# Local-global attention and a gated mixture of attention experts: double steps, one set of PSUM banks, global scores on 544 columns

## The chip, the cores and the metric

The kernel runs on 1 core of one Trainium2 chip. The metric is the device time of one execution in microseconds (us), lower is better.

## The reference

All in fp32. Phase 1, for 8 batches x 8 heads (512 local and 32 global positions, head size 64); `band` keeps |i - j| <= 32:

```
s_g   = scale * q_g @ concat(k_g, k_l).T ;  out_g = softmax(s_g) @ concat(v_g, v_l)
s_l   = concat(scale * q_l @ k_g.T, where(band, scale * q_l @ k_l.T, -1e9))
out_l = softmax(s_l) @ concat(v_g, v_l)
x     = concat(out_g, out_l) over positions, heads side by side      # 8 x 544 x 512
```

Phase 2, per batch, with 4 experts of width 64; each position uses its two best experts:

```
w = softmax of the two largest of x @ w_gate, 0 elsewhere
for e in 0..3:  out += w[:, e] * (softmax(causal(scale * (x@wq[e]) @ (x@wk[e]).T)) @ (x@wv[e])) @ wo[e]
```

## The kernel before

**Work.** Two heads make a pair, four pairs a batch; `PAIRS` lists 32 pairs. For a pair `k`: `p1_load` and `p1_load_values` bring keys, queries and values (POOL copies shifted values and the global ones into windows of 128 rows); `p1_trans` makes `kd` (keys by windows, each followed by the 32 global keys) and `qp`; `p1_scores` (L501) writes `sp`, 32 products of 32 queries with 128 keys in two PSUM banks; `p1_softmax` (L520) is 8 passes on VectorE (L527) and 8 exponentials on ScalarE (L530); `p1_ptrans` (L539) transposes; `p1_av` (L551) gives `xq`; `p1_turn` (L572) transposes it back and `high_low` splits it into `xh` and `xl` for the products of phase 2, which run as three fp32r products (high*high, high*low, low*high). For two pairs together: `p1_global_scores` (L609, `spg`), which scores the global queries against all 640 columns of `kd` (the global keys stand there several times, and `gmask` hides the copies), `p1_global_turn`, `p1_global_av` (`xg`).

For a batch `b`: `m_v` (`pv`), `m_gates`, `m_qk` (`pqk`) for each half `c` of the experts, then per half three tiles `t` of causal scores: `m_scores` (L821, `msp`), `m_softmax` (VectorE, ScalarE, then a multiplication by weight and 1/sum on POOL, L862), `m_ptrans_units` (`mpt` into `mptw`, three buffers), `m_av` (L894, `yp`); `m_tail_scores` and what follows do the last 32 positions; `m_out` (`po`) writes 128 rows.

**Array shapes.** In the profile's rows a TensorE instruction shows rows*columns of the part of the array that it uses: `xq`, `xg`, `yt` 128*32; `sp` 64*32; `msp` 64*64; `spg`, `yp`, `tsp` 128*64; transposes, projections and `po` 128*128; `pg` (the turn of a batch's global keys and queries) 64*128.

**PSUM.** Of the 8 banks, `sc_ring` holds two double ones for `sp` and `msp`, `w_ring` four single ones for all else.

**Order.** The functions only record operations with what they read and write. `Plan.place` (L113) then sets the order: TensorE runs its operations as they were recorded; for the other engines a simulation with estimated times takes, at each moment, the ready operation with the lowest priority number (100 x step, plus `late`). Buffers are rings: an operation waits until its slot comes free. On the chip every engine runs its list in that order, held by semaphores.

**Steps.** `step(s)` (L1038 to L1111) records the work of one step, 42 in all; the pair of phase 1 is `s`, the batch of phase 2 is `b, r = divmod(s - 6, 4)`. TensorE's order in it: `xq` of pair s-2 (with `xg` in odd steps, the tail's `yt` in r = 3), in odd steps `spg` (with `yp` and the tail's scores), `sp` of pair s, one `msp` tile, then `whole(turns, products)`, a run of transposes with projections or output products spread over it, and in r = 0 and 2 a second `msp` tile.

Of the kernel before, what the change touches and what calls it, by code (L numbers as in the profile page):

```python
# [1 line left out]

# [61 lines left out]
class Plan:  # L64
# [48 lines left out]
    def place(self, log=None):  # L113
# [15 lines left out]
        while left:  # L129
# [41 lines left out]
            for b in o.bufs:  # L171
                if b.slot is None:
                    ring = b.ring
                    b.slot = min((s for s in range(ring.n) if ring.slots[s] is not None), key=lambda s: ring.slots[s])
                    ring.slots[b.slot] = None
                    ring.given += 1
                    b.tile = ring.fixed[b.slot] if ring.fixed else b.make()
# [17 lines left out]
def fused_kernel(ctx: ExitStack, tc: tile.TileContext, q_l, k_l, v_l, q_g, k_g, v_g,  # L195
# [34 lines left out]
    def ps(shape, name):  # L230
        return Buf(w_ring, lambda: psum.tile(shape, F32, tag="w", name=name, bufs=4))
# [33 lines left out]
    kds = [const.tile([128, KW], F32, name=f"kd{i}") for i in range(3)]  # L265
    kd_ring = Ring(3, fixed=kds)
# [52 lines left out]

    gmask = const.tile([128, 4, 128], F32, name="gmask")  # L320
# [19 lines left out]

    def setup_gmask():
        def f(e):
            nc.gpsimd.memset(gmask, 0.0)
            nc.gpsimd.memset(gmask[:, 1:, 96:], NEG)
        op("POOL", 800, f, w=["gmask"])
# [27 lines left out]
    X = {}  # L373
# [91 lines left out]
    def p1_trans(k):  # L465
# [5 lines left out]
        qp = buf("qp", [128, SL], 1)  # L471
# [29 lines left out]
    def p1_scores(k):  # L501
# [6 lines left out]
        def f(e):  # L508
            for t in range(4):
                for g in range(4):  # L510
                    u = 4 * t + g
                    c = col(window(u))
                    for h in range(2):
                        rows = slice(64 * h, 64 * h + 64)
                        nc.tensor.matmul(sp.t[32 * g:32 * g + 32, h, 128 * t:128 * t + 128],  # L515
                                         qp.t[rows, 32 * u:32 * u + 32], kd.t[rows, c:c + 128],
                                         start=True, stop=True)
        op("PE", 1100, f, r=[qp, kd], w=[sp])

    def p1_softmax(k):  # L520
# [3 lines left out]
        for h in range(2):  # L524
            for t in range(4):
                i = 4 * h + t
                op("DVE", 211, lambda e, h=h, t=t, i=i: nc.vector.tensor_tensor_reduce(  # L527
                    out=st.t[:, h, t], in0=sp.t[:, h, 128 * t:128 * t + 128], in1=band[:, t], scale=-SCALE, scalar=BIG,
                    op0=ALU.add, op1=ALU.min, accum_out=sm.t[:, 0, i:i + 1]), r=[sp, ("band", t)], w=[(st, i), (sm, i)])
# [9 lines left out]
    def p1_ptrans(k, h):  # L539
# [7 lines left out]
        ptw = buf("ptw", [128, SL], 3)  # L547
# [3 lines left out]
    def p1_av(k):  # L551


        pr = PR[k]
        v, sm = pr["v"], pr["sm"]
# [16 lines left out]
    def p1_turn(k):  # L572
# [8 lines left out]
        if p % 2 == 0:  # L581
            for name in ("xh", "xl"):
                X[b, p // 2, name] = buf(name, [128, 2, S], 3, F32R)
# [3 lines left out]
    def turned(prod, scale, hi_lo, reads):  # L587


        both = buf("turned", [128, 2, D], 1)  # L590
# [18 lines left out]
    def p1_global_scores(b, g):  # L609


        qb = G[b]["qb"]
        sg = buf("long", [128, 5, 128])
        sm = buf("sgm", [128, 8], 3)
        kdl = [PR[b * NP + 2 * g + j]["kd"] for j in range(2)]
        for half in range(2):
            sp = ps([128, 4 - 3 * half, 128], "spg")

            def f(e, half=half, sp=sp):
                for j in range(2):  # L620
                    p, kd, out_ = 2 * g + j, kdl[j].t, sp.t[64 * j:64 * j + 64].rearrange("p c s -> p (c s)")
                    parts = [(out_, kd[:, :512])] if half == 0 else [(out_[:, :96], kd[:, 512:608]),
                                                                     (out_[:, 96:], kd[:, 640:])]
                    for o_, k_ in parts:
                        nc.tensor.matmul(o_, qb.t[:, p, :], k_, start=True, stop=True)  # L625
            op("PE", 950 - 700 * half, f, r=[qb, *kdl], w=[sp])
            if half == 0:
                op("DVE", 610, lambda e, sp=sp: nc.vector.tensor_tensor_reduce(
                    out=sg.t[:, :4], in0=sp.t, in1=gmask, scale=-SCALE, scalar=BIG,
                    op0=ALU.add, op1=ALU.min, accum_out=sm.t[:, 0:1]), r=[sp, "gmask"], w=[(sg, 0), (sm, 0)])  # L630
            else:
                op("DVE", 210, lambda e, sp=sp: nc.vector.tensor_scalar(
                    sg.t[:, 4], sp.t[:, 0], -SCALE, None, op0=ALU.mult, op1=ALU.min, accum_out=sm.t[:, 1:2]), r=[sp],
                   w=[(sg, 1), (sm, 1)])
        op("DVE", 100, lambda e: nc.vector.tensor_reduce(sm.t[:, 2:3], sm.t[:, 0:2], axis=AX.X, op=ALU.min),
           r=[(sm, 0), (sm, 1)], w=[(sm, 2)], late=20)
        op("ACT", 825, lambda e: nc.scalar.activation(sg.t, sg.t, AF.Exp, bias=sm.t[:, 2:3], scale=-1.0,
                                                      accum_out=sm.t[:, 3:4]), r=[sg, (sm, 2)], w=[sg, (sm, 3)], late=30)
# [7 lines left out]
    def long_turn(src, key, where, part):  # L646

        n = 4 - 3 * part
        pa = ps([128, n, 128], "pga")

        def f(e):
            for j in range(n):
                nc.tensor.transpose(pa.t[:, j, :], src.t[:, 4 * part + j], ident)  # L653
        op("PE", 30 + 110 * n, f, r=[src], w=[pa])
# [3 lines left out]
        evac(lambda: pt.t[:, 4 * part:4 * part + n, :], lambda: pa.t, 128 * n, [pa], [(pt, part)])  # L658

    def p1_global_turn(b, g, part):  # L660
        long_turn(G[b, g]["sg"], "pt", G[b, g], part)

    def p1_global_av(b, g):
# [5 lines left out]
        def f(e):  # L669
            for n, w in enumerate((0, 3, 6, 9, NW)):  # L670
                for j in range(2):
                    for h in range(2):
                        c = 64 * j + 32 * h
                        nc.tensor.matmul(xg.t[c:c + 32], pt.t[:, n, c:c + 32], vs[j].t[:, h, w, :],  # L674
# [146 lines left out]
    def m_scores(b, c, t):  # L821
# [4 lines left out]
        def f(e):  # L826
            for i, at in TILES[t]:
                n = 128 * (i + 1)
                for u in range(2):
                    for x in range(2):  # L830
                        rows = slice(64 * x, 64 * x + 64)
                        q0 = 128 * i + 64 * u
                        nc.tensor.matmul(sp.t[64 * u:64 * u + 64, x, at:at + n], qt.t[rows, q0:q0 + 64],  # L833
                                         kt.t[rows, :n], start=True, stop=True)
        op("PE", 160 + 1.67 * sum(128 * (i + 1) for i, _ in TILES[t]), f, r=[kt, qt], w=[sp])

    def m_softmax(b, c, t):
# [5 lines left out]
        for k, (i, at) in enumerate(TILES[t]):  # L843
            n = 128 * (i + 1)
            for x in range(2):
                s = 2 * k + x
                op("DVE", 78 + 1.04 * n, lambda e, x=x, at=at, n=n, i=i, s=s: nc.vector.tensor_tensor_reduce(  # L847
                    out=pm.t[:, x, at:at + n], in0=sp.t[:, x, at:at + n], in1=cmask[:, 384 - 128 * i:512],
# [307 lines left out]
```

## Time and profile before

| | us |
|---|---|
| median of 3 runs (lowest to highest) | 554.78 (554.69 to 556.05) |
| the profiled execution | 553.77 |
| its span, first to last instruction | 552.0 |
| TensorE busy (share) | 512.7 (93%) |
| VectorE busy (share) | 413.8 (75%) |
| ScalarE busy (share) | 323.2 (59%) |
| POOL busy (share) | 287.7 (52%) |
| mean granted TensorE clock | 0.994 |

The span runs from the first to the last instruction; the profiled execution's own time is 1.77 us longer. Busy shares are means over stages with different limits. PE is TensorE's products and PEld its weight loads, which overlap them; DVE is VectorE, ACT ScalarE, SP SyncE. In a timeline two starts that follow each other on one engine tell its pace; the length of a product includes its way through the array, so that lengths overlap.

### The profile page before, as it was taken

Reading aid. Unit: us, or ns where it says so; the run is one execution under the profiler, and the core shown is the slowest. Engines: PE = TensorE matmul, PEld = TensorE weight load, DVE = VectorE, ACT = ScalarE, POOL = GpSimd, SP = SyncE. Lnnn points to the kernel's source line nnn. Section 1 sums busy time; section 2 is a strip of 40 time slices with the busy share of each in tenths; the row PEclk is TensorE's granted clock in tenths of the full one; section 3 lists DMA queues with packets and bytes.
Section 4 is the critical chain, followed back from the end, with each engine's and each line's share of the span. In section 5 each row is a group of like instructions: output and inputs, shape, how many; then the busy total and the mean of one; then the engine's idle time right before and its main releaser. Section 6 shows DMA issues by size and latency. Waiting matters only on the chain.

```text
span 552.0 us, 22219 instructions
## 1 busy us (share of the span) xinstructions
PE 512.7 (93%) x8796; PEld 425.4 (77%) x8796; DVE 413.8 (75%) x1713; ACT 323.2 (59%) x1146; POOL 287.7 (52%) x526
## 2 busy tenths in 40 slices
PE   4887999899999999998999999999999999999976
PEld 3666976778878887887878787788878888788754
DVE  6999879778777887779786896778877775565550
ACT  1767548866466745755675763667457464542552
POOL 6988579874193745648175642927437212231230
PEclk9989999999999999999999999999999999999989
DMA  9786585462262513533163422624122000200202
GB/s 178 144 148 129 111 160 101 86 114 42 53 149 55 95 22 70 146 70 50 25 136 87 84 34 57 145 54 78 22 48 80 2 2 2 78 2 1 77 2 95
DMA packets 190792, 41.83 MB, mean 76 GB/s; under 512 B 186080, under 2 KB 186080, under 8 KB 190688
## 3 DMA queue, kind: packets, MB, share of 16 engines
q1 hardware_dynamic: 174448, 29.12, 28.8%
q10 hardware_dynamic: 16240, 11.29, 6.7%
q8 instruction: 69, 1.13, 0.9%
q14 instruction: 35, 0.29, 0.2%
HBM read 31.47 MB, written 8.91 MB: 73 GB/s over the span
## 4 chain that ended last, share of the span: by engine, by line
PE 65%; DVE 11%; ACT 9%; DMA 5%; POOL 4%; issue 3%; SPq 2%; POOLq 0%; DVEq 0%; ACTq 0%
PE pqk L704 13%; PE pv L741 8%; PE po L984 7%; PE msp L833 6%; PE xq L564 5%; PE mpt L886 5%; PE yp L905 4%; PE sp L515 4%; POOL v L240 3%; PE pt L545 3%; PE spg L625 2%; ACT st L530 2%; DMA v<-in_v_l_dram 2%; PE xp L579 2%; PE pga L653 2%
## 5 line engine op out<-in xcount | busy, mean ns | idle before, releaser
L240 POOL COPY v<-v 32x512 f32<-32x512 f32 (+2 forms) x192 | 116.3, 606 | 46.6 <-DMA v<-in_v_l_dram 36.1
L862 POOL TENSOR_SCALAR pm<-pm,msm,gate 128x512 f32<-128x512 f32 (+3 forms) x128 | 76.9, 614 | 119.8 <-DVE msm L856 86.3
L530 ACT ACTIVATE st<-st,sm 128x128 f32<-128x128 f32 x256 | 100.4, 395 | 35.2 <-DVE sm L527 26.9
L240 POOL COPY v<-vg 32x640 f32<-32x640 f32 (+1 forms) x96 | 65.9, 686 | 38.5 <-PE xg L674 26.8
L851 ACT ACTIVATE pm<-pm,msm 128x512 f32<-128x512 f32 (+3 forms) x128 | 70.6, 554 | 22.9 <-DVE msm L847 22.8
L847 DVE CUSTOM_DVE_ANT_0 pm<-msp,cmask 128x512 f32<-128x512 f32 (+3 forms) x128 | 56.9, 486 | 11.2 <-PE msp L833 11.2
L527 DVE CUSTOM_DVE_ANT_0 st<-sp,band 128x128 f32<-128x128 f32 x256 | 58.1, 285 | 9.4 <-PE sp L515 9.4
L886 PE MATMUL mpt<-ident,pm 128*128 128x128 f32 x320 | 48.1, 276 | 7.1 <-DVE kt L240 3.4
L886 PEld LDWEIGHTS mpt<-ident,pm 128*128 128x128 f32 x320 | 36.5, 141 | 16.2 <-POOL pm L862 5.5
L530 ACT ACTIVATION_READ_ACCUMULATOR st<-st,sm 128x1 f32 x256 | 48.7, 190 | 0.0
L833 PE MATMUL msp<-kt,qt 64*64 64x384 f32 (+3 forms) x512 | 46.1, 448 | 0.5 <-DVE qt L240 0.5
L515 PE MATMUL sp<-kd,qp 64*32 64x128 f32 x2048 | 39.6, 283 | 3.9 <-issue 1.8
L564 PEld LDWEIGHTS xq<-v,ptw 128*32 128x32 f32 x2048 | 30.7, 111 | 14.8 <-issue 6.2
L564 PE MATMUL xq<-v,ptw 128*32 128x64 f32 x2048 | 36.2, 223 | 5.6 <-ACT ptw L238 2.7
L905 PE MATMUL yp<-mptw,vt 128*64 128x128 f32 x640 | 40.1, 278 | 0.3 <-issue 0.3
L704 PE MATMUL pqk<-xh,wk_hi 128*128 128x272 f32 x128 | 39.6, 309 | 0.3 <-DVE xl L604 0.3
L545 PE MATMUL pt<-ident,st 128*128 128x128 f32 x256 | 36.4, 274 | 3.5 <-DVE xl L250 3.2
L704 PE MATMUL pqk<-xh,wq_hi 128*128 128x272 f32 x128 | 39.7, 310 | 0.0
L238 ACT COPY mptw<-mpt 128x512 f32<-128x512 f32 (+1 forms) x51 | 23.9, 487 | 26.2 <-PE mpt L886 25.6
L741 PE MATMUL pv<-wv_hi,xh 128*128 128x260 f32 x128 | 38.6, 301 | 0.7 <-DVE xl L250 0.7
L905 PEld LDWEIGHTS yp<-mptw,vt 128*64 128x64 f32 x640 | 36.2, 139 | 1.7 <-issue 0.7
L704 PE MATMUL pqk<-xl,wq_hi 128*128 128x272 f32 x128 | 36.9, 288 | 0.0
(166 smaller groups left out, 1365.9 us busy)
## 6 DMA issues: line engine op xcount, KB each, us to landing
out_dram<-ot ACTq DMA_DIRECT2D x32, 256.0 KB, 2.1
v<-in_v_l_dram SPq DMA_DIRECT2D x62, 120.0 KB, 3.2
kn<-in_k_l_dram SPq DMA_DIRECT2D x109, 64.0 KB, 2.7
qn<-in_q_l_dram SPq DMA_DIRECT2D x109, 64.0 KB, 2.4
v<-in_v_l_dram SPq DMA_DIRECT2D x59, 32.0 KB, 2.5
vg<-in_v_g_dram SPq DMA_DIRECT2D x21, 64.0 KB, 2.2
qn<-in_q_l_dram ACTq DMA_DIRECT2D x5, 128.0 KB, 2.7
ot<-in_q_g_dram SPq DMA_DIRECT2D x8, 64.0 KB, 2.2
```

The source lines that it names most:

```text
L240: ENG[e].tensor_copy(out, in_)
L515: nc.tensor.matmul(sp.t[32 * g:32 * g + 32, h, 128 * t:128 * t + 128], qp.t[rows, 32 * u:32 * u + 32], kd.t[rows, c:c + 128], start=True, ...
L527: op("DVE", 211, lambda e, h=h, t=t, i=i: nc.vector.tensor_tensor_reduce(out=st.t[:, h, t], in0=sp.t[:, h, 128 * t:128 * t + 128], in1=ban ...
L530: op("ACT", 385, lambda e, h=h, t=t, i=i: nc.scalar.activation(st.t[:, h, t], st.t[:, h, t], AF.Exp, bias=sm.t[:, 0, i:i + 1], scale=-1.0, ...
L564: nc.tensor.matmul(xq.t[32 * g:32 * g + 32, t, h, :], pts[h].t[:, 32 * u:32 * u + 32], v.t[:, h, window(u), :], start=True, stop=True)
L704: nc.tensor.matmul(pp.t, w[:, ch, cols], x(part, ch)[:, n], start=(ch == 0 and w is hi and part == 0), stop=(ch == NCH - 1 and part == 1))
L741: nc.tensor.matmul(pv.t, x(part, ch)[:, 128 * i:128 * i + 128], w[:, ch, :], start=(ch == 0 and part == 0 and w is hi), stop=(ch == NCH - ...
L833: nc.tensor.matmul(sp.t[64 * u:64 * u + 64, x, at:at + n], qt.t[rows, q0:q0 + 64], kt.t[rows, :n], start=True, stop=True)
L851: op("ACT", 280 + 0.83 * n, lambda e, x=x, at=at, n=n, s=s: nc.scalar.activation(pm.t[:, x, at:at + n], pm.t[:, x, at:at + n], AF.Exp, bia ...
L862: op("POOL", 240 + 0.83 * n, lambda e, x=x, at=at, n=n, i=i, s=s: nc.gpsimd.tensor_scalar(pm.t[:, x, at:at + n], pm.t[:, x, at:at + n], sm ...
L886: nc.tensor.transpose(pt.t[:, k, :], pm.t[:, x, at + 128 * j:at + 128 * j + 128], ident)
L905: nc.tensor.matmul(yp.t[64 * x:64 * x + 64, 128 * i:128 * i + 128], vt.t[:, j, 64 * (2 * c + x):64 * (2 * c + x) + 64], flat[:, where[x, i ...
```

## The change

- **Double steps.** `step(d)` records two pairs and half a batch of phase 2; 21 steps in place of 42. TensorE's order: `xq` of both pairs of the step before, `xg` (and `yt`); `sp` of both pairs; `yp` (with the tail's scores), `spg`; a run of 128*128 work; two `msp` tiles; a second 128*128 run, with the transposes of the pairs' scores; one `msp` tile. In step 2 the first batch's `pv` come ahead of the scores of pairs 4 and 5.
- **Banks.** One ring of eight single banks; a score tile takes two of them. Buffers: `kd` 3 to 2; `qp`, `turned` 1 to 2; `ptw` 3 to 4; `mptw` stays at 3.
- **Global scores.** The copies of the global keys in windows 1 to 3 are left out: 416 + 128 columns, no `gmask`; the transposes take blocks of 128, 96, 96, 96 and 128 columns, and the last 32 rows of the first block get a copy of their own.
- **End.** The last batch's tiles come earlier, its multiplications may go to VectorE, its last `yp` is made in two halves, and the tail's output goes first.

Cut to its core:

```diff
-    sc_ring, w_ring = Ring(2, loose=True), Ring(4, loose=True)
+    banks = [psum.tile([128, 512], F32, name=f"bank{i}", bufs=1) for i in range(8)]
+    ring = Ring(8, loose=True, fixed=banks)
...
     def scores(name):
-        return Buf(sc_ring, lambda: psum.tile([128, 2, 512], F32, tag="sc", name=name, bufs=2))
+        return [ps([128, 512], name) for _ in range(2)]
...
     def p1_global_scores(b, g):
...
+                    if half == 0:
+                        parts = [(o_[:, :128], kd[:, :128]),
+                                 (o_[:, 128:].rearrange("p (c s) -> p c s", s=96),
+                                  kd[:, 128:512].rearrange("p (c s) -> p c s", s=128)[:, :, :96])]
+                    else:
+                        parts = [(o_[:, :96], kd[:, 512:608]), (o_[:, 96:], kd[:, 640:])]
+                    for to, k_ in parts:
+                        nc.tensor.matmul(to, qb.t[:, p, :], k_, start=True, stop=True)
...
+    CHUNKS = ((0, 128), (128, 96), (224, 96), (320, 96), (416, 128))
...
     def m_softmax(b, c, t):
...
+                engs = "POOL|DVE" if b == B - 1 and c == 1 else "POOL"
...
+    def step(d):
+        plan.prio = 200 * d
+        odd = d % 2
+        new = (d - 2 - odd) // 2
+        mid, old = new - 1, new - 2
+        pairs = [k for k in (2 * d, 2 * d + 1) if k < NK]
+        done = [k for k in (2 * d - 2, 2 * d - 1) if 0 <= k < NK]
...
+        for k in done:
+            p1_av(k)
+            first.append(lambda k=k: p1_turn(k))
...
+        def scores_of_pairs():
+            for k in pairs:
+                p1_scores(k)
+                p1_softmax(k)
+            if not odd and has(old):
+                m_av(old, 1, M[old, "turn"] if end else None)
+            if odd and has(mid):
+                m_av(mid, 0)
+                m_tail_scores(mid)
+            if pairs:
+                b, p = PAIRS[pairs[0]]
+                p1_global_scores(b, p // 2)
...
+        if odd:
+            first += units((mid, 1, 2), (mid, 1, 1), (mid, 1, 0))
+            if has(new):
+                products = project(0, 2)[:2] if new == 0 else project(new, 1)
+        else:
+            first += units((mid, 0, 1), (mid, 0, 0))
+            if has(old):
+                products = [lambda i=i: m_out(old, i) for i in range(4)]
...
+        if d == 2:
+            whole(first, [])
+            whole([], products)
+            scores_of_pairs()
+        else:
+            whole(first, products, 3 if odd else 0, 0 if odd else 2)
+        if odd:
+            tiles((new, 0, 2), (new, 0, 1))
+        elif mid == B - 1:
+            tiles((mid, 1, 1), (mid, 1, 0))
+        else:
+            tiles((mid, 1, 2), (mid, 1, 1))
...
+        for k in pairs:
+            second += [lambda k=k: p1_ptrans(k, 0), lambda k=k: p1_ptrans(k, 1)]
...
+        if odd:
+            if has(mid):
+                second += [lambda: m_tail_turn(mid, 0), lambda: m_tail_turn(mid, 1)]
+            second += units((new, 0, 2))
+            if has(new):
+                products = project(new, 2)[2 if new == 0 else 0:]
+        elif has(new):
+            products = project(new, 0 if new > 0 else 1)
...
+        whole(second + turned_late, products)
+        if odd:
+            tiles((new, 0, 0), *([(new, 1, 2)] if new == B - 1 else []))
+        elif mid != B - 1:
+            tiles((mid, 1, 0))
```

## Rows read from the trace of the kernel before

**Rows 1.** Part 1 of the page: busy microseconds of each engine, share of the span, instructions.
```profile
PE 512.7 (93%) x8796; PEld 425.4 (77%) x8796; DVE 413.8 (75%) x1713; ACT 323.2 (59%) x1146; POOL 287.7 (52%) x526
```

**Rows 2.** Busy time of each engine in four stretches of the span: start and end, length, then for each engine busy us and instructions, the granted TensorE clock, the DMA engines' share, GB/s.
```profile
0.00:69.00 69.00, 53.75 (x1164) 45.04 (x1167) 58.64 (x258) 39.13 (x158) 53.81 (x104) 0.98 0.75 142
69.00:441.60 372.60, 357.99 (x6534) 297.73 (x6524) 298.40 (x1241) 232.26 (x833) 211.49 (x380) 1.00 0.38 76
441.60:524.40 82.80, 81.43 (x932) 68.08 (x932) 48.21 (x182) 40.80 (x126) 17.61 (x34) 1.00 0.07 27
524.40:552.00 27.60, 19.55 (x189) 14.56 (x184) 8.56 (x34) 10.99 (x32) 4.79 (x8) 0.94 0.14 49
```

**Rows 3.** Part 4 of the page: the chain of work that ended last, by engine.
```profile
PE 65%; DVE 11%; ACT 9%; DMA 5%; POOL 4%; issue 3%; SPq 2%; POOLq 0%; DVEq 0%; ACTq 0%
```

**Rows 4.** What TensorE waited for in 69 to 441.6 us: engine, tile and line that waited, what it waited for, us in total, times, the longest.
```profile
PE mpt L886 <- DVE kt L240: 3.4, 4, 1.2
PE pt L545 <- DVE xl L250: 3.2, 5, 0.6
PE po L984 <- ACT ot L238: 2.4, 4, 0.6
```

**Rows 5.** Timeline, 255.9 to 258.2 us: start, length, engine, line, operation, tiles and shapes, count, and in brackets the idle time before and what ended it.
```profile
256.16 0.29 PE L704 MATMUL pqk<-xl,wq_hi 128*128 128x272 f32 x1
...
257.04 0.43 DVE L240 COPY kt<-pqk 128x272 f32<-128x272 f32 x1
...
257.62 0.41 PE L886 MATMUL mpt<-ident,pm 128*128 128x128 f32 x2 [1.17 <-DVE kt L240]
```

**Rows 6.** Timeline of TensorE, 43.9 to 50.9 us (the columns of group 5, here and in all timelines below).
```profile
44.11 1.10 PE L564 MATMUL xq<-v,ptw 128*32 128x64 f32 x64 [2.05 <-ACT ptw L238]
45.02 0.74 PE L674 MATMUL xg<-v,longt 128*32 128x64 f32 x40
...
50.85 0.39 PE L741 MATMUL pv<-wv_hi,xh 128*128 128x260 f32 x1 [0.67 <-DVE xl L250]
```

**Rows 7.** Timeline of TensorE, 56.8 to 58.9 us.
```profile
56.84 1.10 PE L564 MATMUL xq<-v,ptw 128*32 128x64 f32 x64
57.88 1.16 PE L515 MATMUL sp<-kd,qp 64*32 64x128 f32 x64
```

**Rows 8.** Timeline of TensorE, 257 to 260.6 us.
```profile
259.12 0.29 PE L704 MATMUL pqk<-xh,wq_lo 128*128 128x272 f32 x1
259.24 0.29 PE L704 MATMUL pqk<-xl,wq_hi 128*128 128x272 f32 x1
259.46 1.10 PE L564 MATMUL xq<-v,ptw 128*32 128x64 f32 x64
```

**Rows 9.** Timeline of TensorE, 210 to 213.5 us: the global scores of two pairs, then the products of a batch with its values.
```profile
210.97 1.38 PE L625 MATMUL spg<-kd,qgbd 128*64 128x512 f32 x12
212.13 1.61 PE L905 MATMUL yp<-mptw,vt 128*64 128x128 f32 x25
```

**Rows 10.** Groups of instructions by line and shape: line, engine, operation, tiles, shapes, count, busy us, mean ns of one, idle us before them and what ended it.
```profile
L238 ACT COPY longt<-pga 128x128 f32<-128x128 f32 x18 | 4.8, 267 | 16.1 <-PE pga L653 15.9
```

**Rows 11.** The same view, VectorE.
```profile
L240 DVE COPY mptw<-mpt 128x512 f32<-128x512 f32 x36 | 24.2, 685 | 4.4 <-PE mpt L886 3.7
L568 DVE TENSOR_TENSOR xn<-xq,sm 128x512 f32<-128x512 f32 x32 | 22.0, 687 | 12.2 <-PE xq L564 12.1
...
L498 DVE STREAM_TRANSPOSE qp<-qn 128x512 f32<-128x512 f32 x28 | 19.7, 703 | 0.0
L495 DVE STREAM_TRANSPOSE kd<-kn 128x480 f32<-128x480 f32 x28 | 18.8, 672 | 1.2 <-DMA kn<-in_k_l_dram 1.0
...
L847 DVE CUSTOM_DVE_ANT_0 pm<-msp,cmask 128x256 f32<-128x256 f32 x32 | 12.2, 420 | 0.0
...
L847 DVE DVE_READ_ACCUMULATOR2_ANT msm<- 128x1 f32 x128 | 10.6, 83 | 0.0
...
L847 DVE CUSTOM_DVE_ANT_0 pm<-msp,cmask 128x128 f32<-128x128 f32 x32 | 8.0, 286 | 5.1 <-PE msp L833 5.1
...
L591 DVE TENSOR_SCALAR turned<-xg,sgm 128x128 f32<-128x128 f32 x16 | 5.5, 342 | 0.0
...
L496 DVE STREAM_TRANSPOSE kd<-kn 128x32 f32<-128x32 f32 x28 | 4.7, 168 | 0.0
```

**Rows 12.** Timeline, the last 33 us.
```profile
526.20 1.11 PE L926 MATMUL tsp<-kt,qtbd 128*64 128x512 f32 x8
...
532.86 1.19 PE L886 MATMUL mpt<-ident,pm 128*128 128x128 f32 x6 [2.39 <-POOL pm L862]
...
535.36 1.29 PE L965 MATMUL yt<-vt,longt 128*32 128x64 f32 x40 [0.77 <-DVE longt L240]
...
536.58 3.21 PE L905 MATMUL yp<-mptw,vt 128*64 128x128 f32 x40
...
539.72 0.33 PE L597 MATMUL tt<-ident,turned 128*128 128x128 f32 x1
...
547.96 1.76 ACTq L991 DMA_DIRECT2D out_dram<-ot  x4
```

**Rows 13.** Busy time in 535 to 537 us (the columns of group 2).
```profile
535.00:537.00 2.00, 1.64 (x44) 1.50 (x46) 0.50 (x2) 0.00 (x0) 0.00 (x0) 0.50 0.04 8
```

**Rows 14.** The chain that ended last in order of time, 430 to 445 us: start, us, what.
```profile
436.00 2.23 PE yp L905 x40
```

More of the change, by code (lines that the diff above doesn't have):

```diff
@@ L1 @@
 from contextlib import ExitStack
+import math
 import concourse.bass as bass
@@ L264, in fused_kernel @@
     KW = 32 * (NB + NB // 3)
-    kds = [const.tile([128, KW], F32, name=f"kd{i}") for i in range(3)]
-    kd_ring = Ring(3, fixed=kds)
+    kds = [const.tile([128, KW], F32, name=f"kd{i}") for i in range(2)]
+    kd_ring = Ring(2, fixed=kds)
     NW = NB - 2
@@ L612, in p1_global_scores @@
         qb = G[b]["qb"]
-        sg = buf("long", [128, 5, 128])
+        sg = buf("long", [128, 640])
         sm = buf("sgm", [128, 8], 3)
         kdl = [PR[b * NP + 2 * g + j]["kd"] for j in range(2)]
-        for half in range(2):
-            sp = ps([128, 4 - 3 * half, 128], "spg")
+        for half, n in ((0, 416), (1, 128)):
+            sp = ps([128, n], "spg")
             def f(e, half=half, sp=sp):
                 for j in range(2):
[L621 to L634, printed above, removed]
@@ L892, in m_ptrans_units, with m_av @@
         return units
[L894 removed]
+    def m_av(b, c, between=None):
         vt = M[b, "v"]
         pts = {i: (M[b, c, t, "pt"], M[b, c, t, "where"]) for t in range(3) for i, _ in TILES[t]}
[L897 to L908 removed]
         if c == 0:
@@ L911, in m_av, with f @@
         y = M[b, "yo"]
-        high_low(lambda part: y[part].t[:, c, :], lambda: yp.t, 512, [yp], (y[0], c), (y[1], c))
+        for some in ((0, 1), (2, 3)) if between else (range(4),):
+            n0, n = 128 * some[0], 128 * len(some)
+            yp = ps([128, n], "yp")
+            def f(e, some=some, yp=yp, n0=n0):
+                for i in some:
+                    pt, where = pts[i]
+                    flat = pt.t.rearrange("p a j q -> p (a j) q")
+                    for j in range(i + 1):
+                        for x in range(2):
+                            nc.tensor.matmul(yp.t[64 * x:64 * x + 64, 128 * i - n0:128 * i - n0 + 128],
+                                             vt.t[:, j, 64 * (2 * c + x):64 * (2 * c + x) + 64],
+                                             flat[:, where[x, i, j], :], start=(j == 0), stop=(j == i))
+            op("PE", 235 * sum(i + 1 for i in some), f, r=[vt, *{id(pts[i][0]): pts[i][0] for i in some}.values()], w=[yp])
+            high_low(lambda part, n0=n0, n=n: y[part].t[:, c, n0:n0 + n], lambda yp=yp: yp.t, n, [yp],
+                     (y[0], (c, n0)), (y[1], (c, n0)))
+            if between and n0 == 0:
+                between()
     def m_tail_scores(b):
@@ L954, in m_tail_turn @@
     def m_tail_turn(b, part):
-        long_turn(M[b, "ptail"], (b, "pttail"), M, part)
+        long_turn(M[b, "ptail"], (b, "pttail"), M, part, [(128 * j, 128) for j in range(5)])
     def m_tail_av(b):
@@ L994, in m_out @@
     def m_out(b, i):
-        y = M[b, "yo"]
-        out_tile(y, lambda part, c: y[part].t[:, c, 128 * i:128 * i + 128],
+        y = [(t, (c, n0)) for t in M[b, "yo"] for c in range(2) for n0 in ((0, 256) if b == B - 1 and c == 1 else (0,))
+             if n0 == 0 or i > 1]
+        out_tile(y, lambda part, c: M[b, "yo"][part].t[:, c, 128 * i:128 * i + 128],
                  [(out[b, 128 * i:128 * i + 128, :], slice(0, 128))])
@@ L1002, in m_out_tail, with whole @@
                  [(out[4 * g + r, SL:, :], slice(32 * r, 32 * r + 32)) for r in range(4)])
-    NK = len(PAIRS)
-    LAG = 6
-    def at(k):
-        return 0 <= k < NK
-    def has(b):
-        return 0 <= b < B
-    def whole(turns, products):
-        n = max(len(turns), 1)
+    NK, NG = len(PAIRS), len(PAIRS) // 2
+    def whole(turns, products, last=0, skip=0):
+        n = max(len(turns) - last - skip, 1)
         done = 0
@@ L1117, in fused_kernel @@
     p1_trans(0)
+    p1_trans(1)
     setup_bands()
-    setup_gmask()
     p1_load_values(0)
-    for s in range(LAG + 4 * B + 4):
-        step(s)
+    for d in range(2 * B + 5):
+        step(d)
         for name, when in (("masks", 3), ("v", 1), ("k", 3), ("q", 4), ("o", 6)):
-            if s == when:
+            if d == when // 2:
+                plan.prio = 100 * when
                 setup(name)
```

242 lines of the change are left out of this document (114 added, 128 removed).

## The prediction

> **What bounds the kernel now.** Read the busy times first [rows 1]: TensorE works in 93% of the span, VectorE next. Then the span in four stretches [rows 2]: in the long middle one (69.00 to 441.60) TensorE is busy for 357.99 of 372.60 us at full clock, so 14.6 us are idle; at the start 15.3 of 69.00, in the last 27.60 us 8.0. The chain that ended last [rows 3] is TensorE for 65%. So TensorE in program order is the bound from 69 us on, and a time falls by less work there, by fewer waits inside its order, or at the two ends. VectorE is busy for 298.40 of the same 372.60 us (80%): it is the next bound.
>
> What ends TensorE's waits in the middle [rows 4] is mostly an evacuation: its next product needs a PSUM bank that VectorE or ScalarE has not yet emptied. One of them in order of time [rows 5]: the last projection product starts at 256.16, the copy of `kt` out of its bank starts at 257.04, and only then the transposes of `mpt` go (257.62), though the two `sc` double banks were not needed then.
>
> **The profiled execution** took 553.77 us (span 552.0 and 1.77 around it); the median of the three runs shown is 554.78, 1.0 above. Sums below are differences, set against the median. A measurement of this kernel tells about 0.3% (1.7 us) from no change.
>
> **Part 1, fewer changes of array shape.** Leaving a shape costs TensorE time in which nothing starts. `xq` followed by `xg` of the same shape takes 45.02-44.11 = 0.91 us [rows 6]; the same `xq` followed by `sp` takes 57.88-56.84 = 1.04 [rows 7]: 0.13 for the change. After projection products the next one starts 0.12 us on, after the last one another shape starts 259.46-259.24 = 0.22 on [rows 8]: 0.10. I take 0.10, ends 0.09 and 0.13. How many go away follows from `step`, since TensorE's order is the program's. One batch (four steps before) has 6+5+5+5 = 21 changes: `xq`, then in odd steps the 128*64 products, `sp`, `msp`, the 128*128 run, in r = 0 also `pg` and in r = 0, 2 a second `msp`. After, two double steps: odd `xq, sp, yp/tsp/spg, 128*128, msp, 128*128, msp` = 7, even the same with `pg` = 8. So 15, 6 fewer per batch, 48 in 8 batches, and by the same count 2 more at the ends: 50 x 0.10 = **-5.0 us** (-4.5 to -6.5), all on TensorE.
>
> **Part 2, 544 columns.** The `spg` run takes 212.13-210.97 = 1.16 us [rows 9] for four passes each of 512, 96 and 32 columns, 2560 in all: 0.45 ns per column. The three blocks of 32 masked columns go, 4 x 96 = 384 columns: 0.17 us x 16 = -2.8; four more instructions a run eat a little: **-2.6 us**. No row shows a moving operand that skips columns (96 of every 128): if each of the 288-column passes took twice its 0.13 us, the part would cost 4 x 0.13 x 16 = 8.3 and end at +5.7. I take -2.6, since contiguous ones are all that is near. VectorE's pass over the scores and ScalarE's exponential shrink with the columns, and 16 copies of 267 ns [rows 10] come in for the first block's last 32 rows; these two engines have room, and TensorE has the double step to cover them. Transposes of 96 columns may go faster than the 128 they replace: 0, at best -1.3 (16 x 3 x 0.11 x 1/4).
>
> [...]
>
> **Part 3, waits in the middle.** The bodies with both phases are 13 double steps (d = 3 to 15), so 14.6 us is 1.1 us of idle TensorE per double step. Eight banks in one set take away the waits of [rows 5]'s kind, which [rows 4] put at 3.4+3.2+2.4 = 9.0 us. Products also get further from what they wait for: the transposes of a pair's scores come half a double step after the scores, the last tile's transposes end a whole run. But the head of a double step is new: two `xq`, `xg`, two `sp`, all quick, all filling banks. TensorE runs them in 2 x 0.91 + 0.57 + 1.16 = 3.6 us [rows 6, 7] (0.57: the 40 of `xg` at the pace of the 64 of `xq`) before the second `sp` starts. In that time VectorE must empty the small `msp` tile (2 x 420 + 2 x 286 + 4 x 83 = 1.74 us), two `xq` (2 x 687) and `xg` (342) [rows 11]: 3.5 us. That only just holds, and TensorE's stop there shifts whatever is queued behind it. In even double steps two banks are short besides: `mptw` has three slots, all taken by the second half's tiles until `m_av(old, 1)`, so the transposes of tile (new, 0, 2) stand in PSUM over the step's end. I take 0.8 us per double step in place of 1.1: **-4 us** (-12 with no waits of that kind, +23 by the rival below). VectorE's load rises to about 298/363 = 82%, still under TensorE's.
>
> The queues: SyncE issues the same loads with the same priorities, 16 for a double step's keys and queries, whose two slots come free half a double step before they are needed again; POOL (211.49 of 372.60 us) copies values as before, now for two pairs in a row; ScalarE's queue issues the outputs one by one after their copies. None of them ends a TensorE wait in [rows 4].
>
> **Part 4, start.** Up to 69 us TensorE waits for loads, VectorE (58.64 of 69.00 us busy) and POOL (53.81) [rows 2]. The change puts the first `pv` before pairs 4 and 5. Before, `xq` of pair 3 starts at 44.11 after 2.05 us of idle time and `pv` at 50.85 after 0.67, waiting for its `xl` on VectorE, which has pair 5's softmax as well [rows 6]. With `pv` in front that last idle and that of `sp` go: **-2 us** (-5 to +4: pairs 2 and 3 are now transposed later, and `kd` has two buffers).
>
> **Part 5, end.** [...] The last output was four DMAs, 1.76 us of issuing on ScalarE's queue after 547.96 [rows 12]; now it is one, so three quarters go: 1.3. Half-products of `yp` let its evacuation run beside TensorE: 0.3 to 0.5. Together **-4 us** (-6 to +1).
>
> **Sum:** -5.0-2.6-4-2-4 = -17.6, so 554.8-17.6 = 537 us.
>
> **Rivals.**
> 1. Forecast: 537, own range 529 (part 3 at -12) to 546 (part 3 at 0, the start 5 us later). Chance 0.56.
> 2. The waits only move: a bank is free, but the same VectorE and ScalarE work is late at the head; 1.1 us per double step stay, nothing at the start: 554.8-5.0-2.6-4 = 543. For it: VectorE at 80%, and the waits of [rows 4] end with its work. Chance 0.18.
> 3. Slower: the head of the double step. If VectorE comes there with one pair's transposes (672+168+703 ns) and two 512-column copies (2 x 685) to do [rows 11], 2.9 us late, both `sp` wait as long, in each of 13: idle 38 us in place of 14.6, 543+23 = 566. It decides from (14.6+11.6)/13 = 2.0 us per double step on; at that point the time is 555. Against it: work that is late here is not late again behind. Slower by over 0.3%: 0.14; about even: 0.07.
> 4. The 288-column passes at half speed, the rest as forecast: 537+8.3 = 545. Chance 0.05. [...]
> That the change doesn't do what it says has little room: order and column counts are in the program.
>
> **The numbers.** Faster by over 0.3%: 0.56+0.18+0.05 = 0.79; same 0.07; slower 0.14. The range goes from 527 (the forecast's lower end with part 5 at -6) to 554, which takes in rivals 2 and 4 and the better half of no change.
>
> **What would show it.** Right: 133 or so changes of shape in place of 183 (not counting the value product of the last rows, whose 64 columns show as a change in both); a `spg` run near 1.0 us; TensorE idle about 0.8 us per double step, with few waits on `kt`, `xl` and `ot`; `pv` before the sixth pair's `sp`; full clock in the last 20 us and one issue at the end. Wrong: waits of 2 us and more ahead of the second `sp` or `yp`, ended by VectorE's `xn` or `pm`; a VectorE without idle time in the middle; `spg` above 1.16 us; `pv` later than 51 us.

## The result, and the profile after

The changed kernel takes 559.78 us (median of 14 runs, 555.73 to 563.83), the kernel before 555.39 (14 runs beside it): ratio 1.0079, 95% interval 1.0052 to 1.0105. It is slower by 0.8%; 537 with a range to 554 was predicted. The profiled execution took 559.0 us, its span is 557.2.

Part 1 and part 3 of the page (in part 3: queue, kind, packets, MB, share of the DMA engines), then the same four stretches as [rows 2], the last with its own end:

```profile
PE 505.6 (91%) x8860; PEld 436.0 (78%) x8860; DVE 410.2 (74%) x1732; ACT 318.2 (57%) x1148; POOL 284.9 (51%) x521
...
q8 instruction: 70, 1.15, 0.9%
```
```profile
0.00:69.00 69.00, 53.59 (x992) 44.29 (x992) 53.86 (x235) 32.85 (x136) 56.18 (x108) 0.93 0.75 145
69.00:441.60 372.60, 344.86 (x6377) 301.72 (x6377) 289.58 (x1227) 227.66 (x830) 207.60 (x373) 0.99 0.37 76
441.60:524.40 82.80, 79.16 (x1218) 68.25 (x1218) 53.26 (x222) 41.40 (x141) 16.17 (x32) 1.00 0.04 15
524.40:557.20 32.80, 27.97 (x279) 21.78 (x275) 13.47 (x50) 16.27 (x44) 4.95 (x9) 0.99 0.21 74
```

TensorE has 7.1 us less to do than in [rows 1], 505.6 against 512.7, and the kernel is still slower: TensorE stands still more. In the middle stretch it is idle for 372.60-344.86 = 27.7 us, against 14.6 in [rows 2]. VectorE, which the slower rival had in mind, is busy for less of that stretch than before (289.58 against 298.40).

What TensorE waits for in 104 to 445 us, in the form of [rows 4]. All PSUM tiles are called `bank` now, so the line tells what waits: L522 is `sp`, L689 `xg`, L988 `yt`, L928 `yp`, L575 `xq`.

```profile
PE bank L522 <- issue: 12.1, 10, 1.8
PE bank L689 <- issue: 3.8, 3, 1.4
PE bank L988 <- issue: 2.7, 2, 1.6
PE bank L928 <- issue: 1.3, 3, 0.8
PE bank L575 <- issue: 1.2, 1, 1.2
PE bank L590 <- issue: 0.3, 1, 0.3
```

Not one wait on VectorE or ScalarE is left: the kind of [rows 4] is gone. All that stands here is "issue", time for which the profile shows nothing that TensorE waits for. Over the whole span it is 28 us. The head of one double step, in the columns of the timelines above (the profile has two passes for each of these float32 matmuls, 32 products of a pair's `sp` as `x64` in [rows 7], so `x128` is 64 matmuls):

```profile
186.28 1.00 PE L575 MATMUL bank<-v,ptw 128*32 128x64 f32 x57
187.10 0.67 PE L689 MATMUL bank<-v,longt 128*32 128x64 f32 x33
189.16 0.32 PE L689 MATMUL bank<-v,longt 128*32 128x64 f32 x7 [1.39 <-issue]
189.40 1.96 PE L522 MATMUL bank<-kd,qp 64*32 64x128 f32 x121
192.61 0.42 PE L522 MATMUL bank<-kd,qp 64*32 64x128 f32 x7 [1.25 <-issue]
192.96 1.75 PE L928 MATMUL bank<-mptw,vt 128*64 128x128 f32 x28
```

The stops fall inside a product, in the middle of a tile whose bank is already held: after 33 of the 40 passes of `xg`, after 121 of the 128 of `sp`. From one stop's end to the next one's lie 7+121 = 128 passes and 192.61-189.16 = 3.45 us. Each pass is one weight load and one matmul (2048 of each on L522 in the page), so that is 256 instructions.

Where the time went, from the first `pv` of the second batch and of the last one: before, then after.

```profile
103.02 0.36 PE L741 MATMUL pv<-wv_hi,xh 128*128 128x260 f32 x1
...
480.54 0.37 PE L741 MATMUL pv<-wv_hi,xh 128*128 128x260 f32 x1
```
```profile
109.18 0.39 PE L756 MATMUL bank<-wv_hi,xh 128*128 128x260 f32 x1
...
492.13 0.39 PE L756 MATMUL bank<-wv_hi,xh 128*128 128x260 f32 x1
```

To the second batch +6.2 us; from there to the last 382.9 against 377.5, +5.4; from there to the end of the span 557.2-492.1 = 65.1 against 552.0-480.5 = 71.5, -6.4. The end gained, the start and the middle lost.

At the start TensorE waits twice for nearly 3 us for ScalarE's exponential of the global scores (L643), and after each of these waits the granted clock is low. Timeline around the first, and the clock (the column before the last two) in 71.00 to 75.20 and 92.30 to 95.70:

```profile
71.17 0.77 PE L667 MATMUL bank<-ident,long 128*128 128x128 f32 x5 [2.94 <-ACT long L643]
71.87 3.58 PE L575 MATMUL bank<-v,ptw 128*32 128x64 f32 x128
```
```profile
71.00:75.20 4.20, 4.03 (x133) 3.87 (x137) 1.70 (x4) 0.64 (x4) 0.00 (x0) 0.60 0.71 116
...
92.30:95.70 3.40, 3.40 (x18) 3.40 (x16) 1.32 (x2) 1.11 (x3) 1.16 (x2) 0.50 0.90 190
```

Two `xq` take 3.58 us there, 1.92 in the chain of waits in mid-kernel: at a granted clock of 0.60 in the first window and 0.50 in the second, 1.00 in 185 to 193 us, what follows the pause is stretched too. Ahead of the first `pv` both kernels have low stretches (0.57 in 41 to 49 us, before 0.66 in 36 to 41).

The last 20 us, beside [rows 12, 13]: the wait ahead of `mpt` is 0.24 us (2.39 before), that ahead of `yt` 0.88 (0.77 before), and, as the prediction asked, the clock in 541 to 545 is 1.00 and the last output is one issue of 0.34 us in place of four in 1.76.

```profile
540.18 0.97 PE L904 MATMUL bank<-ident,pm 128*128 128x128 f32 x5 [0.24 <-POOL pm L880]
...
542.89 0.77 PE L988 MATMUL bank<-vt,longt 128*32 128x64 f32 x40 [0.88 <-DVE longt L255]
```
```profile
541.00:545.00 4.00, 3.03 (x66) 2.26 (x66) 2.20 (x8) 0.93 (x6) 0.00 (x0) 1.00 0.00 0
```

### The profile page after: what moved, and what is told of

It is laid out like the page before. It is cut to its first block, busy times and chain, and to the rows that moved or that the text cites. A ratio compares the mean times of both kernels' runs of the same rounds, so it can differ in the third digit from the quotient of the medians.

```text
span 557.2 us, 22376 instructions
## 1 busy us (share of the span) xinstructions
PE 505.6 (91%) x8860; PEld 436.0 (78%) x8860; DVE 410.2 (74%) x1732; ACT 318.2 (57%) x1148; POOL 284.9 (51%) x521
## 3 DMA queue, kind: packets, MB, share of 16 engines
q8 instruction: 70, 1.15, 0.9%
## 4 chain that ended last, share of the span: by engine, by line
PE 84%; issue 6%; DVE 5%; ACT 3%; DMA 1%; POOL 0%; SPq 0%; POOLq 0%; ACTq 0%; DVEq 0%
PE bank L719 16%; PE bank L756 9%; PE bank L1007 9%; PE bank L848 7%; PE bank L928 6%; PE bank L522 6%; PE bank L904 6%; PE bank L575 6%; PE bank L552 4%; PE bank L590 3%; PE bank L636 3%; PE bank L667 3%; PE bank L689 2%; PE bank L767 1%; PE bank L949 1%
## 5 line engine op out<-in xcount | busy, mean ns | idle before, releaser
L862 DVE CUSTOM_DVE_ANT_0 pm<-bank,cmask 128x512 f32<-128x512 f32 (+3 forms) x128 | 55.1, 488 | 19.2 <-PE bank L848 13.4
L534 DVE CUSTOM_DVE_ANT_0 st<-bank,band 128x128 f32<-128x128 f32 x256 | 57.0, 286 | 12.4 <-PE bank L522 11.9
L522 PE MATMUL bank<-kd,qp 64*32 64x128 f32 x2048 | 38.6, 280 | 17.3 <-issue 17.3
L522 PEld LDWEIGHTS bank<-kd,qp 64*32 64x32 f32 x2048 | 30.5, 108 | 22.7 <-issue 21.4
L904 PE MATMUL bank<-ident,pm 128*128 128x128 f32 x320 | 45.4, 276 | 0.8 <-POOL pm L880 0.7
L552 PE MATMUL bank<-ident,st 128*128 128x128 f32 x256 | 39.1, 279 | 4.1 <-ACT st L537 3.4
L848 PE MATMUL bank<-kt,qt 64*64 64x256 f32 (+3 forms) x512 | 41.6, 441 | 0.0
L928 PE MATMUL bank<-mptw,vt 128*64 128x128 f32 x640 | 39.8, 276 | 1.5 <-issue 1.5
L719 PE MATMUL bank<-xh,wq_hi 128*128 128x272 f32 x128 | 39.8, 311 | 0.0
L719 PE MATMUL bank<-xh,wk_hi 128*128 128x272 f32 x128 | 39.4, 308 | 0.0
L928 PEld LDWEIGHTS bank<-mptw,vt 128*64 128x64 f32 x640 | 35.0, 137 | 5.6 <-issue 3.8
L756 PE MATMUL bank<-wv_hi,xh 128*128 128x260 f32 x128 | 38.6, 302 | 0.0
L552 PEld LDWEIGHTS bank<-ident,st 128*128 128x128 f32 x256 | 29.3, 140 | 11.8 <-ACT st L537 8.1
L575 PEld LDWEIGHTS bank<-v,ptw 128*32 128x32 f32 x2048 | 32.5, 118 | 6.9 <-DVE qt L255 2.3
```

Source lines behind the costliest of these rows:

```text
L522: nc.tensor.matmul(sp[h].t[32 * g:32 * g + 32, 128 * t:128 * t + 128], qp.t[rows, 32 * u:32 * u + 32], kd.t[rows, c:c + 128], start=True, ...
L552: nc.tensor.transpose(pt.t[:, t, :], st.t[:, h, t], ident)
L575: nc.tensor.matmul(xq.t[32 * g:32 * g + 32, t, h, :], pts[h].t[:, 32 * u:32 * u + 32], v.t[:, h, window(u), :], start=True, stop=True)
L719: nc.tensor.matmul(pp.t, w[:, ch, cols], x(part, ch)[:, n], start=(ch == 0 and w is hi and part == 0), stop=(ch == NCH - 1 and part == 1))
L756: nc.tensor.matmul(pv.t, x(part, ch)[:, 128 * i:128 * i + 128], w[:, ch, :], start=(ch == 0 and part == 0 and w is hi), stop=(ch == NCH - ...
L848: nc.tensor.matmul(sp[x].t[64 * u:64 * u + 64, at:at + n], qt.t[rows, q0:q0 + 64], kt.t[rows, :n], start=True, stop=True)
```

## The experiments

**Theory F**: TensorE runs out of its own instructions. They come by DMA during the run, 70 packets on queue q8, 1.15 MB or 16.4 KB each: TensorE's 2 x 8860 instructions make 253 a packet, in the kernel before 2 x 8796 in 69 packets 255. A head of `xq`, `xq`, `xg` (`yt`), `sp`, `sp` is 592 to 672 short instructions in one piece; before, the longest such piece was 288. **Theory V**, the prediction's slower rival: VectorE comes late with the banks of the head. A third possibility, that any other order moves the time, is what the last two runs are for.

### The pace of short matmuls by itself

```
for k in range(24): nc.tensor.matmul(warm, a[:, :128], b, ...)   # 512 columns
for k in range(20): sp(short)        # 20 x 32 matmuls in the form of sp
av(wide, 320)                        # in the form of yp
for k in range(10): sp(mixed); av(wide, 16)
for k in range(2): sp(mixed)
```

> Not the reference's computation: loads two tiles, runs matmuls with no wait among them, writes one tile to all of the output. After 24 wide matmuls to warm up: 640 matmuls of the form of sp in one piece (2560 instructions of TensorE), then 320 of the form of yp, then ten times 32 of sp and 16 of yp, then 64 of sp. Theory F: the piece of sp runs at 3.4 to 3.5 us for each 64 matmuls (256 instructions), 34 to 35 us in all, with an idle stretch ended by 'issue' in each block; the piece of yp has none; the mixed piece has next to none. Theory V: 64 of sp take about 2.1 us as in the kernel, 21 us in all, with no idle time, for nothing but TensorE takes part.

Timeline of TensorE in the long piece of `sp` form, then one turn of the mixed piece:

```profile
27.80 2.67 PE L220 MATMUL short<-b,a 64*32 64x128 f32 x175
31.87 2.02 PE L220 MATMUL short<-b,a 64*32 64x128 f32 x128 [1.40 <-issue]
35.87 2.02 PE L220 MATMUL short<-b,a 64*32 64x128 f32 x128 [1.99 <-issue]
...
47.06 2.25 PE L220 MATMUL short<-b,a 64*32 64x128 f32 x128 [0.17 <-issue]
50.51 2.02 PE L220 MATMUL short<-b,a 64*32 64x128 f32 x128 [1.21 <-issue]
...
61.97 1.39 PE L220 MATMUL short<-b,a 64*32 64x128 f32 x81 [1.71 <-issue]
```
```profile
98.37 1.16 PE L220 MATMUL mixed<-b,a 64*32 64x128 f32 x64
99.45 1.97 PE L226 MATMUL wide<-b,a 128*64 128x128 f32 x32
101.35 1.16 PE L220 MATMUL mixed<-b,a 64*32 64x128 f32 x64
```

No product waits for another engine or for a bank, and TensorE stops after every 128 passes exactly. From 31.87 to 61.97 a block of 256 instructions takes 30.10/8 = 3.76 us (3.45 to 4.00), of which some 2.0 are work. The mixed piece passes 192 instructions in 2.98 us, or 256 in 3.97, and does not stop; nor does the wide one. The whole piece took 35.5 us (63.28-27.80, where the wide one starts), a little more than the 34 to 35 of F; a piece without stops would be V's 21. The page has 23 packets on q8 within the run of this small kernel, 0.38 MB or 16.5 KB each; TensorE's 2 x 3056 instructions make 266 a packet, near the 256 (128 pairs) from stop to stop.

```profile
q8 instruction: 23, 0.38, 1.1%
```

When they come is in the trace as well. One block, cut at the start and at the end of its packet (the columns of [rows 2], here without ScalarE):

```profile
31.87:32.97 1.10, 1.10 (x80) 1.10 (x83) 0.00 (x0) 0.00 (x0) 1.00 0.00 0
32.97:34.43 1.46, 0.92 (x67) 0.65 (x48) 0.00 (x0) 0.00 (x0) 1.00 0.06 11
34.43:35.87 1.44, 0.00 (x0) 0.00 (x0) 0.00 (x0) 0.00 (x0) 1.00 0.00 0
```

TensorE goes on at 31.87; the next packet starts 1.1 us later and takes 1.45 (11 GB/s for 1.46 us are its 16 KB); 1.44 us after its end TensorE goes on again. In the nine stops of the piece these three times are 1.05 to 1.13, 0.94 to 1.45 and 1.34 to 1.48 us, so that a block is long where its packet is slow. In the changed kernel each of the 25 stops on "issue" ends 1.2 to 1.6 us after the end of a packet on q8. That is F's mechanism and not only its pace.

### The products put between: the order of the head

```
         def scores_of_pairs():
-            for k in pairs:
-                p1_scores(k)
-                p1_softmax(k)
             if not odd and has(old):
                 m_av(old, 1, M[old, "turn"] if end else None)
...
                 p1_global_scores(b, p // 2)
+            for k in pairs:
+                p1_scores(k)
+                p1_softmax(k)
```

> The changed kernel with one order turned round: in every double step the 128x64 products (yp, tsp, spg) are recorded between the xq/xg products and the scores of the two pairs, and no longer behind these scores. Same instructions, same number of changes of array shape, same eight banks. Theory F (TensorE runs out of its own instructions: a block of 256 of them is not had faster than about 3.45 us, and xq, xg, sp, sp are 592 to 672 short ones in one piece): the run of short ones is cut into 208 to 288 and 256, the idle time of TensorE ended by 'issue' falls from 28 us to 10 to 14 us, and the time from about 559 to 542 to 548 us. Theory V (VectorE frees the scores' banks too late): the scores come later against VectorE's queue, which helps too, 3 to 5 us, but the idle time ended by 'issue' stays over 20 us.

542.64 us, ratio to before 0.9771 (0.9731 to 0.981): 17 us faster than the changed kernel, by order alone. The waits on "issue" went from 28.3 to 12.0 us. TensorE's other named waits grew by 3 us, and its busy time fell from 505.6 to 501.3, with less of the start at the low clock. The largest rows:

```profile
PE bank L689 <- issue: 4.9, 4, 1.5
...
PE bank L522 <- issue: 3.5, 3, 1.7
...
PE bank L988 <- issue: 2.1, 2, 1.1
...
PE bank L575 <- issue: 1.2, 1, 1.2
```

V's small gain, with "issue" still over 20 us, is not what came.

### The same order at the start alone

```
+            early = d < 4
+            if not early:
+                of_pairs()
...
+            if early:
+                of_pairs()
```

> The same order as in the run before, in the first four double steps alone. Global scores then reach ScalarE ahead of the pairs' 16 exponentials. If the two waits of 3 us for the exponential of the global scores at 71 and 92 us, and the low clock behind them, are what the start lost: 5 to 8 us faster than the changed kernel, 551 to 554 us, with the idle time ended by 'issue' in the middle unchanged at some 20 us. If the start lost its time to instructions or to loads: within 2 us of the changed kernel.

558.4 us, ratio 1.0049 (1.0017 to 1.0082): some 1.4 us less than the changed kernel, with overlapping intervals. The waits on the exponential fell from 6.8 to 1.3 us and the clock in 71.00 to 75.20 was 1.00, but 4.3 us of waits on POOL's normalization came in their place:

```profile
PE bank L904 <- POOL pm L880: 4.3, 3, 3.6
...
PE bank L667 <- ACT long L643: 1.3, 1, 1.3
```

The wait was found rightly and its worth was not: behind it stood another. In the trace the second batch comes at 106.74 us, 2.4 earlier than in the changed kernel, where 5 to 8 were expected.

### Longer short runs in the kernel before

```
+        if at(s):
+            p1_scores(s)
+            p1_softmax(s)
         if at(s) and s % 2 == 1:
...
             m_av(old, 1)
-        if at(s):
-            p1_scores(s)
-            p1_softmax(s)
```

> The kernel before with one order turned round the other way: in every step the pair's scores are recorded ahead of spg, yp and tsp, so that in odd steps xq, xg (and yt) and sp stand in one piece of 336 to 416 short instructions. Old PSUM buffers, same number of changes of shape. Theory F: idle time ended by 'issue' appears in odd steps only, 0.5 to 1.4 us in about half of them, 5 to 15 us in all, and the kernel gets slower by 3 to 10 us (558 to 565). Theory V: no idle time of that kind, the time within 2 us of before.

557.91 us, ratio 1.0034 (1.0008 to 1.006), 1.9 us slower: under the 3 to 10 expected, but the waits are there, in the kernel with the old banks, 9.0 us on "issue" in all against 2.6, six of them inside `sp` where there was one:

```profile
PE sp L515 <- issue: 7.6, 6, 1.6
```

Five of the six fell in odd steps, where F puts them (pieces of 336 to 416 instructions do not all hold a whole block); the sixth, in an even step, is the one that the kernel before has. TensorE's other waits are 7 us shorter in all, which hides much of it in the time.

### One more cut

```
+        def narrow():
+            if done:
+                b, p = PAIRS[done[0]]
+                p1_global_av(b, p // 2)
...
                 m_tail_scores(mid)
+            if late:              # d >= 4 and not end
+                narrow()
             if pairs:
```

> As the run with the products between (542.6 us), with xg and yt put behind these products too, ahead of spg: xq, xq | yp, tsp | xg, yt | spg | sp, sp. No piece of short instructions is then longer than 256; two changes of array shape more in each of some 15 double steps. Theory F: idle time ended by 'issue' falls from 12.0 us to 2 to 5 us, the added changes cost 30 x 0.10 = 3 us, so 535 to 541 us. If the rest of those waits were something else than instructions: the 12 us stay and the time is 543 to 547 us.

542.58 us: no gain, against 535 to 541. Waits on "issue" did fall, from 12.0 to 5.6 us. Two rows of the waits that are left:

```profile
PE bank L522 <- issue: 4.1, 8, 1.7
...
PE bank L848 <- DVE qt L255: 3.0, 3, 1.4
```

The trace has 23 more changes of shape, 2.3 us at the 0.10 of part 1; the mixture's scores wait 2.3 us longer for `qt` (0.7 with the order before) and 0.5 longer for ScalarE. That is most of the 6.4 gained, as far as the waits tell. From here on instructions are not the only thing that ends a wait.

### The old division of the banks

```
+    sc_ring, w_ring = Ring(4, loose=True, fixed=banks[:4]), Ring(4, loose=True, fixed=banks[4:])
```

(In the placing of operations, one that needs two banks of a ring also waits until two are free.)

> As the run with the products between (542.6 us), with the eight banks split as in the kernel before: four for scores, four for the rest. Tells what one set of eight is worth. If VectorE's late frees were what bounded the kernel before (part 3 of the prediction): 4 to 10 us slower, with waits of TensorE on VectorE and ScalarE back. Theory F in its strict form, where banks matter little beside instructions: within 3 us of 542.6. In both, idle time ended by 'issue' stays at 10 to 14 us.

554.42 us, ratio 0.9972 (0.995 to 0.9994): 11.8 us slower than with one set of eight (11.2 by the two ratios), more than the 4 to 10 expected. So in this order one set of eight banks is worth what part 3 gave as its far end (-12), and the strict form of F falls: banks matter beside instructions. In the order of the changed kernel their worth was not measured. The waits on "issue" add up to 12.1 us as without the division; six waits on `xl` are back:

```profile
PE bank L1010 <- DVE xl L268: 4.7, 6, 1.0
```

All waits on VectorE are 9.4 us, 3.0 without the division. That names 6.4 of the 11.8; TensorE's busy time is longer too (509.9 against 501.3 for the same instructions), and why stays open.

### 544 columns alone

```
-        for half in range(2):                  # in the kernel before
+        for half, n in ((0, 416), (1, 128)):   # and its products, copies and exponential
```

> The kernel before with the global scores on 544 columns and nothing else of the change. Prediction's part 2: -2.6 us, 552 to 554 us. If moving 96 of every 128 columns halves TensorE's speed: +5.7 us or more, 561. Its spg of 416 columns tells which: about 160 ns a pass if the columns cost the same, about 320 if half speed.

551.75 us, ratio 0.9924 (0.9892 to 0.9956): -4.2 us (-6.0 to -2.4), 2.6 expected. The run of global scores, from its start to that of `yp`:

```profile
213.44 1.23 PE L621 MATMUL spg<-kd,qgbd 128*64 128x128 f32 x16
214.44 2.43 PE L905 MATMUL yp<-mptw,vt 128*64 128x128 f32 x40
```

1.00 us, 1.16 in [rows 9]: 0.16 x 16 = 2.6 us on TensorE, as summed. Moving 96 of every 128 columns shows no cost: four passes each of 128, 288, 96 and 32 columns are 2176, or 0.46 ns per column, 0.45 in part 2. Transposes of 96 columns show a mean of 282 ns in the changed kernel, those of 128 the same, and both start 0.11 us apart: no gain there.

### The start mended

```
-            second += units((new, 0, 2))
+            second += units(*([(new, 0, 2)] if new else []))
-            first += units((mid, 0, 1), (mid, 0, 0))
+            first += units(*([(mid, 0, 2)] if mid == 0 else []), (mid, 0, 1), (mid, 0, 0))
```

> As the run with the products between (542.6 us), but the transposes of the first batch's first mixture tile are moved one half step later (from the end of double step 3 to the head of step 4), since TensorE waits 3.9 us there for GpSimd's normalised probabilities. If that wait is on the path: 2 to 4 us faster (539 to 541). If only the place of the wait moves: within 1 us of 542.6.

536.72 us, ratio 0.9648 (0.9617 to 0.9679): 5.9 us faster than the products between alone, and the best of all here. TensorE reaches the second batch at 104.34 us and the last at 470.48:

```profile
104.34 0.39 PE L756 MATMUL bank<-wv_hi,xh 128*128 128x260 f32 x1
...
470.48 0.39 PE L756 MATMUL bank<-wv_hi,xh 128*128 128x260 f32 x1
```

With the order alone these were 106.39 and 475.08. So 2 us came at the start and another 2.5 between the two, for which no single wait stands and whose cause stays open; the spans differ by 4.5 us, the medians by 5.9.

### Work added at the stop, and elsewhere

```
+    def extra(d):            # double steps 4 to 15
+        for _ in range(2):
+            nc.tensor.matmul(pad.t[:64], ident[:, :64], cmask, start=True, stop=True)
```

> The changed kernel with more work and none moved: in double steps 4 to 15 two matmuls of 128x64 by 512 columns (8 instructions, 4 passes of 0.43 us by the pace of the warm-up passes, 1.72 us) whose result nobody reads stand between xq/xg/yt and the scores of the pairs. 12 x 1.72 = 20.6 us of added work, and 12 changes of shape. Theory F: while the wide passes run the next block of instructions arrives, so the waits of the scores on 'issue' fall by 9 to 14 us and the time grows by 6 to 12 us over 559. Theory V, or any in which the order of the products is what mattered: it grows by 20 to 23 us.

> The control of the run before: the same 20.6 us of added work in the same double steps, but in mid-step, ahead of the mixture's scores, where the trace of the changed kernel shows no wait. Both theories: the waits on 'issue' stay near 28 us and the time grows by 20 to 23 us.

The same 20.6 us of work cost 562.41-559.78 = 2.6 us between `xg` and `sp`, and 582.1-559.78 = 22.3 us in mid-step. By the ratios to before (1.0154, 1.0104 to 1.0205, and 1.0495, 1.0453 to 1.0536, against 1.0079) it is 4.2 and 23.1 us. The waits of `sp`, the first kernel, then the second:

```profile
PE bank L522 <- issue: 3.5, 3, 2.1
```
```profile
PE bank L522 <- issue: 18.1, 14, 2.5
```

The order of the products is that of the changed kernel in both, so order in itself is out, and banks are: a wait for VectorE's frees would also be covered by work put ahead of it, but such waits carry VectorE's name (`xl` with the old banks, 4.7 us), and the small kernel, where no product waits for VectorE, stops too. Eight instructions that take 1.7 us are nearly free where the next block of instructions is awaited: over the whole span the waits on "issue" are 13.1 us, 28.3 without the added work and 27.7 with it in mid-step. That it cost even less than F expected (6 to 12) fits: nearly all of the stops at `sp` were covered, 3.5 us being left of 17.3.

## Why the prediction was wrong

**Part 1** (-5.0) stands as far as it can be seen: by TensorE's order in the trace, without the value product and the new steps between 96 and 128 rows inside `xg` and `pga`, which cost next to nothing (the 40 passes of `xg` start within 0.53 us, 0.52 without them), there are 133 changes, as forecast, against 183. The 0.10 us for one was not measured alone.

**Part 2** (-2.6) was right in sign and mechanism, -4.2 measured alone, with 2.6 inside the interval; the half-speed rival is out.

**Part 3** (-4) is the step that failed. It had the right place, the head of the double step, and looked there for VectorE's frees. The premise under it was that TensorE runs `xq`, `xq`, `xg` and the first `sp` in 3.6 us, at paces read from [rows 6, 7], where 104 and 128 passes stand in a row. Pieces that short say nothing of one of 296 and more: in the double step shown above, from the start of `xq` (185.29, outside the rows) to that of `yp` (192.96) lie 7.67 us, 2.64 of them in two stops. Between the first `pv` of the second batch and that of the last TensorE stands idle for 382.95-358.70 = 24.3 us in the changed kernel, nearly all of it on "issue", and for 377.52-365.81 = 11.7 before: +12.5 where -4 stood. The waits on evacuations did go, as was said of the eight banks; waits for instructions came in their place, and the other order of the head does without 16 us of them. In numbers the slower rival's 566 was near, by the wrong engine.

A row of before could have told: TensorE's longest wait without a named releaser stands inside an `sp`, after 61 of its 64 passes, and cost 1.80 us.

```profile
98.33 1.12 PE L515 MATMUL sp<-kd,qp 64*32 64x128 f32 x61
101.25 0.41 PE L515 MATMUL sp<-kd,qp 64*32 64x128 f32 x3 [1.80 <-issue]
```

It was passed over because [rows 4] were read from the largest sums down. At this stop the bank is held, the profile names no operand that was late, and a packet on q8 ends 1.3 us before TensorE goes on.

**Part 4** (-2) had the first `pv` right (49.25 us against 50.85) and missed what follows: the second batch comes 6.2 us later. TensorE pauses twice for 2.8 to 2.9 us for the exponential of the global scores, and the clock is low after each. That exponential stands behind the two pairs' 16 on ScalarE, and it needs a small reduction on VectorE (L641) that ran at 68.81 and 90.47 us, 8 and 10 us after VectorE had read the scores; the first time ScalarE's copies of `ptw` held it until 70.25 besides. Which of these is at the root the runs do not separate. They do show that with the pairs' scores recorded later the wait shrinks, that POOL's takes part of its place, and that with both out of the way the second batch comes at 104.34: 4.8 us earlier, still 1.3 later than before the change.

**Part 5** (-4) was right in direction and about in size. Of the four it works out 1.3 for the issues and estimates 0.3 to 0.5 for the half-products; no run shows the other 2.2 to 2.4 as a term by itself. What the runs showed in their place is a wait of 0.24 us ahead of `mpt`, a clock of 1.00 and 6.4 us less from the last batch on, of which 3.3 are idle time of TensorE and 3.1 its busy time, so that some of parts 1 and 2 is in it.

Together, by the spans of the two traces and the first `pv` of the second and of the last batch:

| | forecast | changed kernel | head and start in the other order |
|---|---|---|---|
| to the second batch (part 4) | -2 | +6.2 | +1.3 |
| from there to the last (parts 1 to 3, nearly all) | -11.6 | +5.4 | -11.4 |
| from there to the end (part 5) | -4 | -6.4 | -6.3 |
| span | -17.6 | +5.2 | -16.4 |

In the middle of the changed kernel TensorE's busy time fell by 365.81-358.70 = 7.1 us, close to the 7.6 of parts 1 and 2; it is part 3 that is out by 16.5 us, and the start by 8.2. That the other order takes 536.72 us, and so meets the forecast of 537, is in part luck: it has waits for instructions (13.4 us) that the forecast left out, and the order may have gains of its own.

## What to carry to other kernels

Count a piece of short instructions, not only its columns: here 256 of TensorE's were not to be had faster than 3.45 us, and 600 in a row at 8 ns each cost up to two stops, while the same products with wide ones between them stopped for 12 us in all in place of 28. A wait on "issue" that begins in the middle of a tile is the sign, and work added there that costs next to nothing (here 2.6 us for 20.6) is the proof. When a step is made twice as long, follow the first rounds by hand on every engine: what was covered by the other half is bare there.

## What the runs showed of the hardware

Instructions come by DMA during the run, 70 packets of 16.4 KB on q8 in the changed kernel; in the small kernel TensorE stopped every 128 pairs of weight load and matmul, 3.45 to 4.00 us apart, with no other DMA traffic beside the packets. That time is 1.05 to 1.13 us from TensorE's going on to the start of the next packet, 0.94 to 1.45 of the packet itself, which makes the difference, and 1.34 to 1.48 from its end to TensorE. What sets each of the three stays open, as does whether other engines meet it. A moving operand of 96 of every 128 columns cost no more than one without gaps (0.46 ns per column over the `spg` run, 0.45 before), and a transpose of 96 columns took as long as one of 128 (a start every 0.11 us).
